# Loading an FFN weight as whole rows in two DMAs instead of four column pieces

## The chip, the cores and the metric

The kernel runs on one core of a Trainium2 chip. The metric is the time of one execution on the device in microseconds; before the change it is 184.65 us, the median of three runs (184.38 to 184.68). Beside those runs there is one profiled execution, of which the profile and the trace tell.

## What is computed

A linear attention with sketched features for 4 batches of 4 heads (1088 positions, 32 dimensions a head), and behind it a feed-forward network on the 4352 rows of 128 that come out of it:

```
phi(x) = outer(S1 x, S2 x), 64 features
num = phi(q) (phi(k)^T v);  den = phi(q) sum(phi(k)) + 1e-6
x   = num / den              # 4352 x 128
h   = max(x @ w_in, 0)       # w_in: 128 x 2048
out = (h * h) @ w_out        # w_out: 2048 x 128
```

All inputs and the output are float32. w_in and w_out are 1 MB each.

## The kernel before

The work is a stream of FFN units with the attention of the next positions worked in between. `FC` cuts the 4352 positions into ten column chunks (256, 384, 448, 448, five of 512, 256). A chunk has 16 blocks of 128 hidden columns; they are grouped into units of one or two blocks. For a unit, PE multiplies a 128 x 128 block of `w_in` with the chunk's `xT` (`ffn1`, L597, into a PSUM tile `pg`), ACT takes the maximum with zero (L609) into `gt`, ACT or DVE squares it (L620, L622) into `g`, and PE multiplies with a block of `w_o` and adds up in PSUM (`ffn2`, L641, tile `po`). The first unit reads blocks 0, so the first 128 columns of `w_in` and `w_o`.

The order of the main part is worked out when the kernel is built, by the class `_Order` from given durations. What comes before it, up to the first 256 positions of `xT`, is written out by hand, and so are the first loads. In that prologue:

- DMAs are issued by SP, one after the other, in the order of the code: k, q and v of the first batch, then (behind `load_q(nc.sync, 0, 256, 640)`) the weights, then the rest of q (`load_q(nc.sync, 0, 640, S)`), and then k, v and q of the second batch. Tiles are `kn`, `qn` and `vn`; a DMA of `vn` writes 32 partitions, one of `kn` or `qn` all 128. SP uses eight semaphores in turn, so a DMA is issued only when the eighth before it has landed.
- `w_in` comes from memory in four pieces of 512 columns (`load_wi`, L208), 128 partitions with 2 KB each, into `w_in32`. `w_o` comes in four pieces as well (`load_wo`, L213), each of 512 rows of `w_out`, put side by side on 128 partitions in runs of 512 bytes. The pieces alternate in the queue: w_in 0, w_in 1, w_o 0, w_in 2, w_o 1, w_in 3, w_o 2, w_o 3.
- POOL copies `w_in32` into `w_in`, in the type that PE reads, in four casts of 512 columns (`cast_wi`, L685). Each cast reads all 128 partitions of its columns. The casts stand in POOL's order behind its setup work and ahead of the small copies `rd` (L510) that the second part of the first batch needs.
- PE works through the sketch of k (`kf`, `kvp`), denominators and numerators of the first 256 positions (`den`, `num`), two small groups on tile `x`, one warm matmul that reads the first 512 columns of `w_in` (L835), and then the first four FFN matmuls (L597). DVE makes `xT` for them (L844).

```
    for c in range(4):
        cast_wi(c)
...
    for _ in range(W3):
        nc.tensor.matmul(st["warm"][:, :], w_in[:, 0:128], w_in[:, 0:512])
```

Of the kernel before, what the change touches and what calls it, by code (L numbers as in the profile page):

```python
# [14 lines left out]
def _ap(t: bass.AP, p0: int, np_: int, off: int, free):  # L15
    p = list(t.ap)[0]
    return bass.AP(
        t.tensor, t.offset + p0 * p[0] + off, [[p[0], np_]] + [list(d) for d in free]
    )
# [88 lines left out]
def kernel(  # L108
# [11 lines left out]
    nc = tc.nc  # L120
# [39 lines left out]
    def sb(name, cols, dt=F32, rows=128):  # L160
        return cpool.tile([rows, cols], dt, tag=name, name=name)
# [9 lines left out]
    w_in32, w_o, w_in = sb("w_in32", 2048), sb("w_o", 2048), sb("w_in", 2048, F32R)  # L171
# [14 lines left out]
    def load_q(eng, b, c0, c1):  # L186
        eng.dma_start(
            qn[b % 2][:, c0:c1],
            bass.AP(q.tensor, q.offset + b * H * S * D + c0, [[G * D, 128], [1, c1 - c0]]),
        )  # L190
# [13 lines left out]
            ),  # L204
        )

    def load_wi(eng, c):
        eng.dma_start(  # L208
            w_in32[:, 512 * c : 512 * c + 512], moe_w_in[:, 512 * c : 512 * c + 512]
        )  # L210

    def load_wo(eng, c):
        eng.dma_start(  # L213
            _ap(w_o, 0, 128, 512 * c, [[128, 4], [1, 128]]),
            bass.AP(
                moe_w_out.tensor, moe_w_out.offset + c * 512 * 128,
                [[128, 128], [128 * 128, 4], [1, 128]],
            ),
        )

# [484 lines left out]
        )  # L705
    nc.scalar.copy(ss[:, :], sp[:, 0:80])
    load_q(nc.sync, 0, 256, 640)
    load_wi(nc.sync, 0)
    load_wi(nc.sync, 1)
    load_wo(nc.sync, 0)  # L710
    load_wi(nc.sync, 2)
    load_wo(nc.sync, 1)
    load_wi(nc.sync, 3)
    for c in range(2, 4):
        load_wo(nc.sync, c)
    load_q(nc.sync, 0, 640, S)
    keep_warm(W1)
    a_kT0(0, 2)
# [348 lines left out]
    for u in range(NU):  # L1067
        ci, c0, n, d0, m = units[u]
# [93 lines left out]
```

## Time and profile before

| | |
|---|---|
| median of three runs | 184.65 us |
| profiled execution | 184.44 us, its span 182.6 us |
| PE busy | 177.6 us, 97% of the span |
| DVE, ACT, POOL busy | 67%, 74%, 21% |
| granted TensorE clock | 0.998 of full speed |
| DMA | 24610 packets, 11.26 MB |
| w_in, four DMAs of 256 KB | issue to landing 4.0 to 5.4 us, median 4.2 |
| w_o, four DMAs of 256 KB | issue to landing 4.9 to 6.1 us, median 5.6 |

Times in the profile are from the span's start. A busy PE is one with a matmul in its pipeline. In the row of tenths each digit is the busy share of one of 40 slices of 4.6 us. A line of the timeline gives start, length, engine, source line, operation, tile written and tile read, count, and in brackets how long the engine had been idle and what released it; several like instructions are merged. The timeline shows `w_in32` and `w_in` both as `w_in`, since buffer numbers are left out.

### The profile page before, as it was taken

Reading aid. Unit: us, or ns where it says so; the run is one execution under the profiler, and the core shown is the slowest. Engines: PE = TensorE matmul, PEld = TensorE weight load, DVE = VectorE, ACT = ScalarE, POOL = GpSimd, SP = SyncE. Lnnn points to the kernel's source line nnn. Section 1 sums busy time; section 2 is a strip of 40 time slices with the busy share of each in tenths; the row PEclk is TensorE's granted clock in tenths of the full one; section 3 lists DMA queues with packets and bytes.
Section 4 is the critical chain, followed back from the end, with each engine's and each line's share of the span. In section 5 each row is a group of like instructions: output and inputs, shape, how many; then the busy total and the mean of one; then the engine's idle time right before and its main releaser. Section 6 shows DMA issues by size and latency. Waiting matters only on the chain.

```text
span 182.6 us, 3995 instructions
## 1 busy us (share of the span) xinstructions
PE 177.6 (97%) x1529; PEld 104.7 (57%) x1529; DVE 122.2 (67%) x262; ACT 136.0 (74%) x258; POOL 39.2 (21%) x158
## 2 busy tenths in 40 slices
PE   8899999999999999999999999999999999999992
PEld 2768876755645655555455554545555555555792
DVE  3979969999999961799994335996353334333640
ACT  3339679749948886799937778894777777777990
POOL 5535418438300002570018100500000000000000
PEclk9999999999999999999999999999999999999999
DMA  5899994010029500000030200003003000300111
GB/s 155 220 266 341 221 266 105 4 32 0 0 47 260 157 0 4 4 2 0 0 54 15 43 0 5 0 0 59 0 4 57 0 0 5 52 0 0 32 29 29
DMA packets 24610, 11.26 MB, mean 62 GB/s; under 512 B 17936, under 2 KB 23056, under 8 KB 24592
## 3 DMA queue, kind: packets, MB, share of 16 engines
q1 hardware_dynamic: 24272, 10.89, 24.5%
q8 instruction: 12, 0.20, 0.5%
q10 hardware_dynamic: 320, 0.13, 0.3%
q14 instruction: 6, 0.05, 0.1%
HBM read 8.78 MB, written 2.23 MB: 60 GB/s over the span
## 4 chain that ended last, share of the span: by engine, by line
PE 95%; DMA 2%; DVE 0%; SPq 0%; issue 0%; ACT 0%; ACTq 0%
PE po L641 61%; PE pg L597 18%; PE nd L550 3%; PE po L636 2%; PE pol L636 2%; DMA kn<-in_k_dram 2%; PE qc L303 2%; PE nd L414 1%; PE kvp L396 1%; PE qc L347 1%; PE kvp L414 1%; PE x L756 1%; PE kf L315 0%; PE nd L347 0%; DVE kt L290 0%
## 5 line engine op out<-in xcount | busy, mean ns | idle before, releaser
L641 PE MATMUL po<-g,w_o 128*128 128x512 f32 (+3 forms) x288 | 122.7, 547 | 0.2 <-PE pg L597 0.2
L609 ACT ACTIVATE gt<-pg 128x512 f32<-128x512 f32 (+3 forms) x144 | 75.2, 570 | 31.5 <-PE pg L597 31.0
L641 PEld LDWEIGHTS po<-g,w_o 128*128 128x128 f32 x288 | 53.4, 189 | 32.3 <-issue 24.8
L597 PE MATMUL pg<-xT,w_in 128*128 128x512 f32 (+3 forms) x160 | 70.2, 519 | 0.0
L620 ACT ACTIVATE g<-gt 128x512 f32<-128x512 f32 (+2 forms) x102 | 60.7, 623 | 1.6
L622 DVE TENSOR_TENSOR g<-gt 128x512 f32<-128x512 f32 (+3 forms) x43 | 30.4, 708 | 39.5 <-ACT gt L609 38.8
L597 PEld LDWEIGHTS pg<-xT,w_in 128*128 128x128 f32 x160 | 29.2, 190 | 28.5 <-ACT gt L609 11.6
L510 POOL COPY rd<-rc 32x9 f32<-32x9 f32 (+2 forms) x80 | 19.5, 243 | 26.4 <-DVE rc L502 23.2
L456 POOL COPY kv<-kvt 32x64 f32<-32x64 f32 x48 | 12.7, 264 | 44.7 <-DVE kvt L433 42.5
L519 DVE STREAM_SHUFFLE qa<-qc 128x576 f32<-128x576 f32 (+2 forms) x20 | 11.8, 646 | 0.0
L534 DVE TENSOR_TENSOR qp<-qa,qb 128x576 f32<-128x576 f32 (+2 forms) x20 | 10.8, 602 | 0.0
L482 DVE STREAM_TRANSPOSE qt<-qc 128x576 f32<-128x576 f32 (+2 forms) x10 | 5.8, 608 | 6.0 <-PE qc L347 4.3
L367 DVE TENSOR_TENSOR kp<-fs 128x576 f32<-128x576 f32 x12 | 8.7, 742 | 0.0
L645 DVE STREAM_TRANSPOSE oT<-po 128x512 f32<-128x512 f32 (+3 forms) x9 | 5.9, 651 | 2.1 <-PE po L641 2.1
L550 PE MATMUL nd<-qp,kv 32*32 32x288 f32 (+2 forms) x320 | 6.6, 354 | 0.0
L519 DVE STREAM_SHUFFLE qb<-qc 128x576 f32<-128x576 f32 (+2 forms) x10 | 6.1, 649 | 0.0
L567 DVE TENSOR_TENSOR xT<-nd,bc 128x576 fp32r<-128x576 f32 (+2 forms) x10 | 5.6, 589 | 0.6 <-PE nd L550 0.5
L636 PE MATMUL po<-w_o,g 128*128 128x128 f32 x32 | 5.8, 279 | 0.0
L296 DVE STREAM_TRANSPOSE qT<-qn 128x192 f32<-128x192 f32 (+3 forms) x11 | 5.7, 549 | 0.0
L636 PE MATMUL pol<-w_o,g 128*128 128x128 f32 x32 | 5.7, 275 | 0.0
L560 DVE STREAM_TRANSPOSE bc<-rd 128x576 f32<-128x576 f32 (+2 forms) x10 | 5.6, 593 | 0.0
L550 PEld LDWEIGHTS nd<-qp,kv 32*32 32x32 f32 x320 | 2.9, 103 | 3.6 <-issue 2.4
(106 smaller groups left out, 89.8 us busy)
## 6 DMA issues: line engine op xcount, KB each, us to landing
kn<-in_k_dram SPq DMA_DIRECT2D x3, 544.0 KB, 8.8
qn<-in_q_dram SPq DMA_DIRECT2D x3, 544.0 KB, 8.7
vn<-in_v_dram SPq DMA_DIRECT2D x9, 144.0 KB, 6.4
w_in<-in_moe_w_in_dram SPq DMA_DIRECT2D x4, 256.0 KB, 4.2
w_o<-in_moe_w_out_dram SPq DMA_DIRECT2D x4, 256.0 KB, 5.6
out_dram<-oT SPq DMA_DIRECT2D x12, 64.0 KB, 1.9
out_dram<-oT SPq DMA_DIRECT2D x8, 56.0 KB, 1.8
out_dram<-oT SPq DMA_DIRECT2D x8, 48.0 KB, 1.8
```

The lines of the kernel that those rows point to most:

```text
L367: nc.vector.tensor_tensor(out=_ap(st[b, "kp"], 0, 128, 64 * NT * h, [[64, NT], [8, 8], [1, 8]]), in0=_ap(fs, 0, 128, o, [[32, NT], [1, 8], ...
L456: nc.gpsimd.tensor_copy(_ap(st[b, "kv"], 32 * c, 32, 64 * h, [[32, E], [1, 32]]), _ap(st["kvt"], 32 * h, 32, 0, [[64, E], [1, 32]]),)
L510: nc.gpsimd.tensor_copy(st[b, "rd", i0][32 * h : 32 * h + 32, n * c : n * c + n], st["rc"][32 * c : 32 * c + 32, n * h : n * h + n],)
L519: nc.vector.stream_shuffle(in_=banks(st[b, "qc", i0], 2 * x, 0, m), out=_ap(st[b, which, i0], 0, 128, 2 * m * x, [[m, 2], [1, m]]), mask=m ...
L534: nc.vector.tensor_tensor(out=st[b, "qp", i0, e][:, r], in0=st[b, f"qa{e}", i0][:, r], in1=st[b, "qb", i0][:, r], op=mult,)
L550: nc.tensor.matmul(nd[32 * h : 32 * h + 32, 512 * c : 512 * c + m], kv[r, o : o + 32], qp[r, m * h : m * h + m], start=(e == 0), stop=(e = ...
L597: nc.tensor.matmul(st["pg", u][:, n * i : n * i + n], w_in[:, 128 * (d0 + i) : 128 * (d0 + i) + 128], xT[:, c0 : c0 + n],)
L609: nc.scalar.activation(gt[:, 0:w], st["pg", u][:, 0:w], Relu)
L620: nc.scalar.activation(to, of, Square)
L622: nc.vector.tensor_tensor(out=to, in0=of, in1=of, op=mult)
L636: nc.tensor.matmul(po[x // 128][:, 0:128], g[:, x : x + 128], w, start=(d == 0), stop=(d == NB - 1),)
L641: nc.tensor.matmul(po[0][:, 0:n], w, g, start=(d == 0), stop=(d == NB - 1))
```

## The change

`w_in32` is loaded as whole rows: one DMA for partitions 0 to 79 and one for partitions 80 to 127, each with all 2048 columns (8 KB a row). Both stand ahead of all of `w_o`, which follows as two pieces of 512 rows and one of 1024. The four casts stay as they are. The weights so come in five DMAs instead of eight. In the built kernel the first cast waits for both DMAs of `w_in` and the other three casts wait for nothing more; the order of instructions on PE, DVE, ACT and POOL is the same.

```
-    def load_wi(eng, c):
+    def load_wi(eng, c, n=1):
+        r = slice(512 * c, 512 * (c + n))
+        for p in (slice(0, 80), slice(80, 128)):
+            eng.dma_start(w_in32[p, r], moe_w_in[p, r])
+
+    def load_wo(eng, c, n=1):
         eng.dma_start(
-            w_in32[:, 512 * c : 512 * c + 512], moe_w_in[:, 512 * c : 512 * c + 512]
-        )
-
-    def load_wo(eng, c):
-        eng.dma_start(
-            _ap(w_o, 0, 128, 512 * c, [[128, 4], [1, 128]]),
+            _ap(w_o, 0, 128, 512 * c, [[128, 4 * n], [1, 128]]),
             bass.AP(
                 moe_w_out.tensor, moe_w_out.offset + c * 512 * 128,
-                [[128, 128], [128 * 128, 4], [1, 128]],
+                [[128, 128], [128 * 128, 4 * n], [1, 128]],
             ),
         )
...
     load_q(nc.sync, 0, 256, 640)
-    load_wi(nc.sync, 0)
-    load_wi(nc.sync, 1)
+    load_wi(nc.sync, 0, 4)
     load_wo(nc.sync, 0)
-    load_wi(nc.sync, 2)
     load_wo(nc.sync, 1)
-    load_wi(nc.sync, 3)
-    for c in range(2, 4):
-        load_wo(nc.sync, c)
+    load_wo(nc.sync, 2, 2)
     load_q(nc.sync, 0, 640, S)
```

## The prediction

> **What bounds the kernel now.** I read the page's busy shares first, then the timeline of PE, POOL and DVE around the first FFN matmul, then the queue of SP's DMA issues, and last the rates of other loads later in the trace.
>
> The page:
>
> ```profile
> PE 177.6 (97%) x1529; PEld 104.7 (57%) x1529; DVE 122.2 (67%) x262; ACT 136.0 (74%) x258; POOL 39.2 (21%) x158
> ...
> PE   8899999999999999999999999999999999999992
> ...
> DMA  5899994010029500000030200003003000300111
> ```
>
> PE is busy for 97% of the span and from about 15 us on has no gap worth naming, so whatever moves the start of the FFN moves the end by the same amount. The DMA engines are full only in the first seven slices (to about 27 us), and there the weights are loaded. So the change is decided before 15 us. POOL and then PE in that stretch (start, length, engine, line, what):
>
> ```profile
> 10.43 1.35 POOL L685 CAST w_in<-w_in 128x512 fp32r<-128x512 f32 x2 [3.24 <-DMA w_in<-in_moe_w_in_dram]
> 13.42 0.61 POOL L685 CAST w_in<-w_in 128x512 fp32r<-128x512 f32 x1 [1.64 <-DMA w_in<-in_moe_w_in_dram]
> 15.19 0.61 POOL L685 CAST w_in<-w_in 128x512 fp32r<-128x512 f32 x1 [1.16 <-DMA w_in<-in_moe_w_in_dram]
> ```
>
> ```profile
> 12.30 0.49 PE L835 MATMUL warm<-w_in 128*128 128x512 f32 x1
> 12.64 0.70 PE L597 MATMUL pg<-xT,w_in 128*128 128x256 f32 x4
> ...
> 13.71 0.47 PE L597 MATMUL pg<-xT,w_in 128*128 128x256 f32 x2
> 14.41 0.67 PE L641 MATMUL po<-g,w_o 128*128 128x256 f32 x2 [0.22 <-PE pg L597]
> ```
>
> The first cast starts at 10.43, as soon as the first column chunk lands, and ends 0.61 later at 11.04. Its first reader on PE, the warm matmul, starts only at 12.30, because the matmuls before it in PE's order end at 12.37. The first FFN matmul at 12.64 waits for xT, which DVE ends at 12.53:
>
> ```profile
> 12.11 0.42 DVE L844 TENSOR_TENSOR xT<-num,bc 128x256 fp32r<-128x256 f32 x1
> ...
> 13.48 1.16 DVE L622 TENSOR_TENSOR g<-gt 128x256 f32<-128x256 f32 x2
> ```
>
> So w_in's first chunk has about 1.2 us to spare, and nothing on PE waits for w_in today. SP's queue of issues:
>
> ```profile
> 5.92 0.43 SPq L187 DMA_DIRECT2D qn<-in_q_dram  x1
> 6.40 0.90 SPq L208 DMA_DIRECT2D w_in<-in_moe_w_in_dram  x2
> 7.34 0.43 SPq L213 DMA_DIRECT2D w_o<-in_moe_w_out_dram  x1
> 7.82 1.40 SPq L208 DMA_DIRECT2D w_in<-in_moe_w_in_dram  x1
> ```
>
> **What is removed.** Eight weight DMAs become five, 0.43 to 0.51 us of SP's time each, so three of them save some 1.4 us of SP. This buys nothing: the transfers are served in order behind each other and DMA stays at 9 tenths, so the queue is never short of work. The loads behind the weights (qn from column 640, kn and vn of the second batch) are issued earlier, but stand behind the same bytes. They have slack: qn lands 6.1 us after its issue at 11.32, so at 17.4, and its transposes start at 19.50; kn lands at 20.7 and its transposes start at 21.62. I cost them at nothing. If the whole weight stream ended over 0.9 us later, kn would be the next late thing; the bytes are the same, so I do not expect it. The order on PE, DVE, ACT and POOL is unchanged.
>
> **What is added: one wait in place of four.** A row-wise DMA carries all columns of some partitions, and each cast reads all partitions, so the first cast now waits for both w_in DMAs, 1.05 MB, where it waited for one chunk of 0.26 MB. Behind it in POOL's queue stand only the other three casts (then nothing until the `rl` copies at 16.61). They run back to back, one every 0.74 us (two took 1.35). With T the landing of the second w_in DMA they end at about T + 0.66, 1.40, 2.14 and 2.88.
>
> How late may T be? The FFN matmuls of 256 columns follow each other every 0.12 us, so the warm matmul of 512 columns needs about 0.24 us of PE. With 0.1 us from a releaser to PE (xT's end at 12.53 to the matmul at 12.64) the first cast may end at 12.64 - 0.24 - 0.1 = 12.3 without cost, so T may be 12.3 - 0.66 = 11.64. Beyond that PE waits at the warm matmul, and everything behind it in PE's order (the four matmuls of `pg`, the sketch of q, the rest) is late by T - 11.64. The later casts do not add: chunks 1, 2 and 3 are first read at 13.71, 15.39 and 17.61, so with the delay they have until T + 2.07, 3.75 and 5.97.
>
> **When does T come?** The trace has no 8 KB rows and no load of 80 or 48 partitions, so I bound it, landing to landing. The load ahead of w_in is qn, issued at 5.92, landed 2.7 later, at 8.6. Behind it, 1.05 MB at three rates of this trace:
>
> ```profile
> 56.00:57.00 1.00, 1.00 (x4) 0.60 (x4) 0.96 (x3) 0.97 (x3) 0.00 (x0) 1.00 0.98 402
> 57.70:58.60 0.90, 0.90 (x4) 0.58 (x4) 0.90 (x2) 0.67 (x2) 0.00 (x0) 1.00 1.08 209
> 60.00:60.60 0.60, 0.60 (x4) 0.23 (x3) 0.60 (x3) 0.60 (x2) 0.00 (x0) 1.00 1.02 413
> ```
>
> These windows (last column GB/s) are later loads with no weights among them: kn, then vn, then qn. kn and qn cover 128 partitions with long rows and run at 402 and 413 GB/s. vn covers 32 partitions per DMA and falls to 209; its four DMAs, issued at 54.47, 54.89, 55.36 and 55.84, land 4.1, 4.4, 4.5 and 4.4 later, so the last three (410 KB) take from 58.6 to 60.25, 250 GB/s.
> - Fast end: at 425 GB/s (qn's 557 KB in the 1.3 us after vn's last landing), 1.05 MB take 2.5 us: T = 11.1.
> - vn's rate, 250 GB/s: 4.2 us, T = 12.8.
> - Slow end: today's first two chunks, 524 KB, land at 11.1 (issued at 6.87, 4.2 later), 2.5 us after qn, 210 GB/s: 5.0 us, T = 13.6.
>
> I take a little better than vn, 260 GB/s: 4.0 us, T = 12.6. vn is the nearest row because it is the only load here that leaves partitions out, and the two new DMAs do so too, though less (80 and 48 against 32); the long rows pull the other way, towards kn. Both ends stay in the range. Delay: 12.6 - 11.64 = 1.0 us.
>
> [...]
>
> **A small gain back.** Two DVE squares of one shape, 256 columns each, differ:
>
> ```profile
> L622 DVE TENSOR_TENSOR g<-gt x2: 413/618/824, 13.5 to 14.2; 128x256 f32<-128x256 f32 x2
> ```
>
> The first, 0.82 us from 13.48, lies beside the cast at 13.42 to 14.03; the second, beside no cast, takes 0.41. PE waited 0.22 us for the first (`po` at 14.41). With the change, the first FFN matmul is at T + 1.0 and this square, 0.84 later, at T + 1.84, in the third cast (to T + 2.14): it loses 0.3 us instead of 0.4 or more. The second then meets the fourth cast, but its reader (15.15 today, against its end at 14.64) has 0.5 to spare. I take 0.1 us of gain, between none and 0.22.
>
> **Sum.** +1.0 - 0.1 = +0.9 us. The profiled execution took 184.44 us, 182.6 of span and 1.84 around it, which does not change: 185.34. It lies 0.21 under the median of the runs, 184.65, so the median comes to 185.5. PE's later work passes the delay on whole, as it has no gaps that could swallow it.
>
> **Rivals.**
> - *Not slower: the long rows are fast.* If the 1.05 MB land within 3.0 us of qn (345 GB/s or more), T is at most 11.64 and the wait is hidden as today's is. For it: kn and qn run at 402 and 413 GB/s, and from 7.8 to 9.6 us, with almost only w_in's 2 KB pieces in the queue, the load moved 218 GB/s, so the column pieces themselves may be what is slow. Against it: neither DMA covers the 128 partitions that kn and qn do. Time: 184.65 less 0 to 0.22, that is 184.4 to 184.65; to be faster by more than 0.37 us the earlier end of the casts would have to help the q chain on DVE too, whose `pd` (15.23) stood beside the fourth cast, and PE behind it has little to give. [...]
> - *Slower still: T at 13.2 or later.* The row-wise form keeps today's 210 GB/s, or one of the DMA engines lags (an instruction fetch shares them; the third w_in issue took 1.40 instead of 0.43), and the first cast now waits for the last engine of both DMAs. That T does come at today's rate is also what happens if the 8 KB rows are cut into 2 KB packets. T = 13.6 gives +1.96 - 0.1: 186.5.
> - *w_o becomes the wait.* Its first quarter now stands behind all of w_in. At 250 GB/s it lands at T + 1.05, and its first reader (14.41 plus the delay) comes at T + 2.77. It would decide only if the quarter took 2.8 us, under 100 GB/s; the half that is loaded last has 4 us of cover. Chance 2 in 100, counted with the slower case.
>
> **How the numbers follow.** 0.2% is 0.37 us, about what a measurement of this kernel can tell. My case, T from 12.1 to 13.2 (+0.4 to +1.5 us): 0.48. Slower still: 0.22. Not slower: 0.30, of which 0.20 lies within 0.37 us and 0.10 below. So slower 0.70, same 0.20, faster 0.10. The range goes from the fast end, 184.4, to the slow end and a little, 186.8.
>
> **What would show it.** In the profile after: the first cast starts at T, at 12.6 (12.1 to 13.2), with its wait of 3.2 us grown to about 5.4, and the other three follow without a wait; the warm matmul on w_in starts some 0.7 us behind the first cast's start instead of at 12.30, and PE has a new gap of about 1 us just before it; xT still ends near 12.5; the first square on DVE is shorter than 0.82. Packets fall from 24610 by 512 and rise by 128, to 24226. From 20 us on, each FFN matmul is late by the same 0.9. I am wrong if the first cast starts before 11.7 (no loss), if PE waits at `po` for w_o, or if kn's transposes at 21.62 begin to wait for their load.

## The result, and the profile after

The changed kernel takes 190.48 us (median of 6, 189.64 to 190.96) against 184.47 for the kernel before (6 runs): a ratio of 1.0315, 95% interval 1.0284 to 1.0347. That is 6.0 us slower; forecast were 0.9 us and a range up to 186.8. The direction was right, the size was not. The profiled execution took 190.94 us, its span 189.2. In three of the kernels below the profiled execution was a slow one (188.09, 207.91 and 467.26 us, against medians of 185.47, 185.71 and 186.75), so no time is read from those three profiles, only when loads landed and what had to wait for them.

The page after (busy shares, PE's tenths, the granted clock in tenths, the packets, the chain by line):

```profile
PE 180.4 (95%) x1529; PEld 107.2 (57%) x1529; DVE 121.7 (64%) x262; ACT 136.4 (72%) x258; POOL 38.7 (20%) x158
...
PE   8955999999999999999999999999999999999992
...
PEclk9996699999999999999999999999999999999999
...
DMA packets 24178, 11.26 MB, mean 60 GB/s; under 512 B 17888, under 2 KB 23008, under 8 KB 24032
...
PE po L641 59%; PE pg L597 18%; DMA w_in<-in_moe_w_in_dram 5%; PE nd L550 3%; PE po L636 2%; PE pol L636 2%; DMA vn<-in_v_dram 2%; PE qc L303 2%; PE nd L414 1%; PE qc L347 1%; PE kvp L414 1%; SPq L199 1%; PE warm L831 0%; PE nd L347 0%; POOL w_in L685 0%; ACTq L221 0%
```

PE has a hole in slices three and four (9.5 to 18.9 us), w_in's DMA now stands on the chain with 5%, and the clock row, all nines before, has two sixes right behind the hole. POOL and PE at that place in the timeline, the line numbers of the written-out prologue four lower than before on PE:

```profile
15.81 2.28 POOL L685 CAST w_in<-w_in 128x512 fp32r<-128x512 f32 x4 [8.62 <-DMA w_in<-in_moe_w_in_dram]
```

```profile
12.04 0.50 PE L440 MATMUL x<-kvt,irep 32*128 32x128 f32 x8 [0.34 <-ACT sw L826]
16.47 0.79 PE L831 MATMUL warm<-w_in 128*128 128x512 f32 x1 [3.93 <-POOL w_in L685]
17.07 1.06 PE L597 MATMUL pg<-xT,w_in 128*128 128x256 f32 x4
```

The first cast starts at 15.81 instead of 10.43. PE waits 3.93 us at the warm matmul, and the first FFN matmul comes at 17.07, 4.43 us late. But the FFN is later than that in the end: matched one to one, the matmuls from 22 us on start 6.34 us after their counterparts of before, and it stays so to the end. The other 1.9 us arise between 17 and 22 us. Three windows after (the columns behind the engines are the granted clock, the DMA share and GB/s) show why:

```profile
12.40:15.70 3.30, 0.14 (x8) 0.00 (x0) 0.59 (x2) 0.37 (x1) 0.00 (x0) 1.00 1.13 256
15.75:22.58 6.83, 6.11 (x49) 5.00 (x50) 4.64 (x23) 4.07 (x8) 4.02 (x13) 0.50 1.07 296
22.60:30.00 7.40, 7.40 (x127) 6.04 (x125) 4.42 (x12) 4.91 (x10) 1.44 (x8) 1.00 0.92 232
```

In the first PE is idle. In the second, 6.83 us long, it works at a granted clock of 0.50; only then is the clock back at 1.00.

So there are two losses: w_in lands late, and PE is slow after the wait. The experiments split the first and test the second.

### The profile page after: what moved, and what is told of

It is laid out like the page before. It is cut to its first block, busy times and chain, and to the rows that moved or that the text cites. A ratio compares the mean times of both kernels' runs of the same rounds, so it can differ in the third digit from the quotient of the medians.

```text
span 189.2 us, 3993 instructions
## 1 busy us (share of the span) xinstructions
PE 180.4 (95%) x1529; PEld 107.2 (57%) x1529; DVE 121.7 (64%) x262; ACT 136.4 (72%) x258; POOL 38.7 (20%) x158
## 2 busy tenths in 40 slices
DMA packets 24178, 11.26 MB, mean 60 GB/s; under 512 B 17888, under 2 KB 23008, under 8 KB 24032
## 4 chain that ended last, share of the span: by engine, by line
PE 89%; DMA 6%; SPq 1%; POOL 0%; ACTq 0%; issue 0%; DVE 0%; POOLq 0%
PE po L641 59%; PE pg L597 18%; DMA w_in<-in_moe_w_in_dram 5%; PE nd L550 3%; PE po L636 2%; PE pol L636 2%; DMA vn<-in_v_dram 2%; PE qc L303 2%; PE nd L414 1%; PE qc L347 1%; PE kvp L414 1%; SPq L199 1%; PE warm L831 0%; PE nd L347 0%; POOL w_in L685 0%; ACTq L221 0%
## 5 line engine op out<-in xcount | busy, mean ns | idle before, releaser
L641 PE MATMUL po<-g,w_o 128*128 128x512 f32 (+3 forms) x288 | 124.0, 552 | 0.0
L641 PEld LDWEIGHTS po<-g,w_o 128*128 128x128 f32 x288 | 54.4, 193 | 31.9 <-issue 24.5
L597 PE MATMUL pg<-xT,w_in 128*128 128x512 f32 (+3 forms) x160 | 71.8, 531 | 0.0
L597 PEld LDWEIGHTS pg<-xT,w_in 128*128 128x128 f32 x160 | 30.6, 199 | 28.6 <-ACT gt L609 11.5
```

The source lines that it names most:

```text
L597: nc.tensor.matmul(st["pg", u][:, n * i : n * i + n], w_in[:, 128 * (d0 + i) : 128 * (d0 + i) + 128], xT[:, c0 : c0 + n],)
L641: nc.tensor.matmul(po[0][:, 0:n], w, g, start=(d == 0), stop=(d == NB - 1))
```

## The experiments

All are made from the changed kernel unless said otherwise, and compared with the kernel before on the same chip, whose median was 184.29 to 184.68 us. Kernels measured on different chips are compared by their ratios. For landings I use the trace's increments of a DMA's semaphore, one per DMA engine: "fifteen engines" is the last of all but the latest.

**Whole rows in one DMA.**

```
-        for p in (slice(0, 80), slice(80, 128)):
+        for p in (slice(0, 128),):
```

> The changed kernel with w_in's whole rows in one DMA over all 128 partitions instead of 80 and 48. Theory A (a DMA that leaves partitions out moves slowly, whatever its rows): the rows run at kn's rate, 345 to 425 GB/s behind qn, w_in lands at 11.1 to 12, the first cast starts there instead of at 15.8, PE has no gap before the warm matmul, the granted clock stays at 1.0, and the time is 184.4 to 185.0 us. Rival B (8 KB rows as such are slow, in a DMA of any shape): the first cast still starts at 14.5 or later and the time is 188.5 to 190.5 us. Rival C (it is the order, w_in whole ahead of the casts): first cast at 13 to 14, time 186 to 188 us.

Measured: 187.31 us, ratio 1.0140 (1.0117 to 1.0164). The rows are the same 8 KB, but w_in lands on fifteen engines at 11.45 and on the last at 12.58, against 14.32 and 15.69 with 80 and 48. An 8 KB packet takes 0.309 us at the median, against 0.553. Theory B, that long rows are slow as such, is refuted, and theory A holds for fifteen engines. Its time does not: the sixteenth engine is 1.13 us behind, and after a wait of only 0.78 us at the warm matmul the clock falls here too. The time is in the range of rival C, but the cast at 12.64 is not, and the order by itself, tested below, is worth 0.1% or nothing. PE's waits and the window behind them:

```profile
PE warm L831 <- POOL w_in L685: 0.8, 1, 0.8
```

```profile
14.00:18.00 4.00, 4.00 (x46) 3.18 (x45) 3.75 (x16) 3.08 (x7) 1.68 (x7) 0.58 1.09 321
```

**Two DMAs of 64 and 64.**

```
-        for p in (slice(0, 80), slice(80, 128)):
+        for p in (slice(0, 64), slice(64, 128)):
```

> The changed kernel with the two row-wise DMAs of 64 and 64 partitions instead of 80 and 48. Theory A: partitions 0 to 63 and 64 to 127 are each served at about the rate of vn's DMAs (230 to 250 GB/s), so the two take 2.1 to 2.3 us each, one after the other; w_in lands for most engines near 13 and for the last one near 14 to 15.5, time 188 to 190.5 us. [...] Rival B (8 KB rows as such): same as the changed kernel, 190 to 191 us.

Measured: 189.78 us, ratio 1.0273 (1.0224 to 1.0321), packets 0.581 us. With equal halves an 8 KB packet takes no less than with 80 and 48 (0.553), so the unequal split is not what makes it slow. w_in lands on fifteen engines at 14.38, later than the 13 that vn's rate gave.

**Three DMAs, the first across the middle.**

```
-        for p in (slice(0, 80), slice(80, 128)):
+        for p in (slice(32, 96), slice(0, 32), slice(96, 128)):
```

> The row-wise load in three DMAs: partitions 32 to 95, then 0 to 31, then 96 to 127. The first has as many rows as the first DMA of the 64/64 run (64), but from both halves of the partitions. Theory A1 (what counts is whether a DMA reaches both the lower and the upper 64 partitions): its 64 rows land for most engines at 9.7 to 10.3 and for the last near 11, an issue to landing of 4.2 to 4.8 us against 5.8 for partitions 0 to 63; the two DMAs of 32 behind it are slow (1.1 us each); first cast at 13 to 14, time 187.5 to 189 us. Theory A2 (what counts is the number of partitions in a DMA): the first DMA takes as long as partitions 0 to 63 do, issue to landing 5.6 to 6.0 us, and the first cast starts at 14.5 or later, 189.5 us or more.

Measured: 189.34 us, ratio 1.0288 (1.0256 to 1.0321). This tells the number of partitions from their place. Both this kernel's first DMA and that of the 64/64 run have 64 rows. Issue to landing of the DMAs on w_in, first of this kernel, then the 64/64 run; in both the shortest is the first DMA:

```profile
DMA to landing us min/median/max: 6.9/7.0/7.2
```

```profile
DMA to landing us min/median/max: 5.8/6.7/7.6
```

Read to the last engine, partitions 32 to 95 (6.9) look worse than 0 to 63 (5.8), against theory A1. But 6.9 is one engine, at 13.24. The other fifteen land at 10.00 to 11.50, half of them by 10.3, those of the 64/64 run at 10.19 to 12.02, half by 11.6. In the packets it is plainest: once running, those of partitions 32 to 95 take 0.309 us like those of the full DMA, and those of the two DMAs of 32 partitions behind it 0.44 and 0.57 at the median. So with 64 rows it is the place that counted (0.309 us a packet across the middle, 0.581 with a half on each side), as in A1; the time that I gave for it missed, since I had not counted the late engine.

**The split by itself, with columns again** (eight DMAs; the first cast waits for two of them).

```
-    load_wi(nc.sync, 0, 4)
+    for c in range(4):
+        load_wi(nc.sync, c)
```

> The other half of the change alone: the split into 80 and 48 partitions, but by column pieces again (eight DMAs of 512 columns, all ahead of w_o), so that the first cast waits for the first two only. Theory (the partial DMAs slow the whole of w_in, but the loss reaches PE only since the first cast waits for all of it): the last of w_in lands at 13 to 15, as in the changed kernel, the first two pieces of 256 KB at 10.5 to 11.6; first cast under 11.7, time 184.4 to 185.5 us with at most a short gap at the first matmul on w_o. Rival (runs of 8 KB are what is slow in the changed kernel, not the split): all of w_in lands by 12.5.

Measured: 185.71 us, ratio 1.0063 (1.0043 to 1.0083). The last of w_in lands at 14.55, as late as expected, yet the first cast starts at 10.80 and costs nothing: PE waited for the slow form only where the first cast waits for all of it (3.93 us in the changed kernel). The time misses the range by 0.2. Of the 1.4 us of loss, about 0.5 is at the first matmul on w_o, which now stands behind eight DMAs: PE waits 0.75 us there, where it waited 0.22 before. The rest I did not trace. The landings come from loads, which do not wait for PE.

**Order alone** (four column pieces of 128 partitions, all ahead of w_o).

```
-    load_wi(nc.sync, 0, 4)
+    for c in range(4):
+        load_wi(nc.sync, c)
```

(with `load_wi` as it was before, the pieces of w_o as in the change)

> The kernel before with only the order of the change: four pieces of w_in by columns, all ahead of w_o, which follows as two quarters and a half. Theory A (the order is harmless, the row-wise DMAs are the loss): the first cast starts at 10.4 to 10.8, the casts of chunks 2 and 3 by 13, no new wait on PE, time 184.2 to 184.8 us. Rival C (w_o behind all of w_in is late for the first matmul on it at 14.41, or the merged half of w_o is): a gap at that matmul, time 185 to 187 us.

Measured: 184.89 us, ratio 1.0010 (0.9984 to 1.0037). Moving w_o back costs little. The gap of rival C is there, in small (PE's waits; at this matmul it waited 0.22 us before the change):

```profile
PE po L640 <- DMA w_o<-in_moe_w_out_dram: 0.8, 1, 0.8
```

**Two halves by columns**, 128 partitions and 4 KB runs.

```
-    load_wi(nc.sync, 0, 4)
+    load_wi(nc.sync, 0, 2)
+    load_wi(nc.sync, 2, 2)
```

(with `load_wi` as before, over n pieces)

> w_in in two DMAs of 1024 columns over all 128 partitions (4 KB runs) ahead of w_o, which follows as in the changed kernel. Theory: runs of 4 KB over all partitions move at the rate of the single DMA, so the first half lands at 10.2 to 11.2 with the late engine, under the 11.64 that cost nothing, and the second by 12.7, ahead of its first reader at 15.4: no new gap on PE, the granted clock stays 1.0, time 184.2 to 184.8 us, at best 0.2 us under the kernel before. Rival: w_o's first quarter, now behind all of w_in, is late for its matmul at 14.41 as in the run with four column pieces first (0.5 us): 184.9 to 185.4 us.

Measured: 184.88 us, ratio 1.0018 (0.9993 to 1.0044). The first cast starts at 11.31 and PE does not wait for it, only 0.27 us for w_o at the matmul that the rival names. The clock stays at 1.00, and nothing is gained: w_in's earlier end has no one who needs it. The time lies between the ranges of theory and rival. This form is not told apart from the kernel before.

**PE kept busy through the wait.**

```
+    keep_warm(18)
     for _ in range(W3):
         nc.tensor.matmul(st["warm"][:, :], w_in[:, 0:128], w_in[:, 0:512])
```

> The changed kernel with 18 more matmuls on constants (512 columns of bf16 each, some 0.21 us each, their result is not used) between PE's last matmul on tile x and the warm matmul on w_in, so that PE is busy while it waits. Theory: of the 6 us lost, 4.05 us are the wait for w_in and some 2 us are FFN work at the lower granted clock (0.58 and 0.74 from 15 to 25 us) that follows PE's idle 4 us. Then the first cast still starts at 15.8, the granted clock stays at 1.0 and the time is 188.3 to 188.8 us. Rival (the lower clock costs nothing, since ACT or DVE set the pace after 17 us, and the whole loss is the wait): time within 0.5 us of 190.5.

Measured: 189.31 us, ratio 1.0248 (1.0225 to 1.0271). The first cast starts at 15.53, hardly earlier, but the clock row is nines throughout, and from 16 to 33 us of the old timeline the FFN matmuls are 4.04 us late instead of 6.34. The same window as in the changed kernel:

```profile
15.75:22.58 6.83, 6.83 (x68) 5.34 (x67) 4.99 (x24) 5.25 (x11) 4.16 (x15) 1.00 1.07 266
```

So the lower clock costs about 2.3 us. The two starts are not quite alike: w_in lands 0.28 us sooner here, and the warm matmul starts only when the added ones are done (16.57), not as soon as the cast ends (16.14). In the time only 1.2 us of the 2.3 appear, so the theory's 188.3 to 188.8 is missed: near 41 us PE stops once for about 0.5 us in the middle of `nd` with nothing to wait for,

```profile
PE nd L550 <- issue: 0.5, 1, 0.5
```

behind which the FFN stays 0.7 us later. I take it for a side effect of the added PE instructions; that was not tested.

**The same in the kernel with one DMA**, where the wait is short: four matmuls instead of 18.

> The kernel with w_in in one DMA over 128 partitions, and four more matmuls on constants (512 columns of bf16, 0.21 us each) on PE ahead of the warm matmul on w_in, which fill the 0.8 us that PE waits there. Theory: that wait alone, 0.8 us, makes the granted clock fall to half for 3.4 us and costs 1.2 us of the 2.6; filled, the clock stays at 1.0 and the time is 185.6 to 186.3 us. Rival: so short a wait does not move the clock, which fell for PE's thin work before it; it falls again, 187.0 to 187.6 us.

Measured: 185.82 us, ratio 1.0072 (1.0052 to 1.0092). Without them the ratio is 1.0140, so they are worth 0.7%, 1.3 us; matched one to one, the FFN is 0.91 us later than before with them and 2.2 us later without. The same window as above, with 0.58 there, has 1.00 here:

```profile
14.00:18.00 4.00, 4.00 (x54) 3.22 (x53) 3.54 (x18) 3.79 (x8) 1.55 (x7) 1.00 1.08 327
```

The wait of 0.78 us of PE at this place is thus dearer in its clock (1.3 us) than in itself.

**The late engine.** In the changed kernel and in the kernels with one and with three DMAs, one DMA engine lands w_in 0.8 to 1.4 us behind the other fifteen (0.2 with 64 and 64, where the others are late themselves). In the profiles with unshifted instructions a fetch of 16 KB of instructions, one packet of 0.9 to 1.3 us, starts at 7.9 to 8.7 us, just as w_in begins. I took that for the cause and moved the fetch, first in the kernel with one DMA:

```
-    keep_warm(W0)
+    keep_warm(8 * W0, 64)
...
-    keep_warm(W1)
+    keep_warm(8 * W1, 64)
```

> The kernel with w_in in one DMA over 128 partitions, and PE's two groups of warm matmuls at the start cut into eight times as many of 64 columns (40 and 24 instead of 5 and 3 of 512), so that PE's instruction stream is 112 instructions longer ahead of w_in at about the same PE time. Theory: the one DMA engine that lands 1.1 us behind the other fifteen (12.58 against 11.04 to 11.45) is the one that carries a 16 KB instruction fetch at 7.9 us, taken 0.9 to 1.3 us; with more instructions ahead the fetch comes at 5.5 to 7 us, before w_in's bytes, the last engine lands w_in at 11.5 to 11.8, the first cast starts there instead of at 12.64, and the time falls from 187.3 to 184.6 to 185.6 us. Rival: that engine is late for another cause; the first cast stays at 12.4 to 12.8 and the time at 186.9 to 187.6 us.

Measured: 185.47 us, ratio 1.0068 (1.0050 to 1.0087), by the ratios 1.3 us better than without the shift, within the range of the theory. But the profile does not show its mechanism: the fetch came at 6.03 as planned, and the last engine landed 0.2 us behind the next instead of 1.13, yet all of them landed later (up to 12.90); the issue of w_in's DMA, beside the fetch, took 1.26 us instead of 0.43. In the four other runs the mean clock was 0.998 to 1.000, where the kernel with one DMA has 0.991 in all four: the gain, as large as that of filling the wait, may be the clock's. Then with a further shift (twelve more matmuls) and PE's wait filled:

> The kernel with w_in in one DMA over 128 partitions, with the small warm matmuls at the start (40 and 36 of 64 columns, 136 PE instructions more than before) and the four constant matmuls that fill PE's wait. In the run with 112 more the profiled fetch came at 6.0 us and met the issue of the w_in DMA (1.26 us instead of 0.43), so this one moves it further, to 5 to 5.9 us. Theory (the late DMA engine is the one that carries PE's instruction fetch): w_in lands on the last engine at 11.3 to 11.8, less than 0.6 us behind the others, the first cast starts by 11.9, the clock stays at 1.0, and the time is 184.4 to 185.2 us, against 185.8 with the filling alone. Rival (late for another cause): first cast at 12.3 to 12.6 again, 185.6 to 186.2 us.

Measured: 186.75 us, ratio 1.0114 (1.0082 to 1.0147), slower than with the filling alone. The theory's time is missed, and its landings too: with the fetch at 6.97, w_in lands on fifteen engines at 11.71 and on the last at 14.37, 2.66 us behind. And in the changed kernel itself:

> The changed kernel itself (80 and 48 partitions) with the earlier fetch and with eleven constant matmuls in PE's wait. If the three causes add up (partial DMAs, one late engine, the lower clock), the first cast starts at 13.9 to 14.6 instead of 15.8, the clock stays at 1.0, and the time is 186.9 to 187.9 us: the partial DMAs alone, 2.5 to 3.3 us over the kernel before. Rival (the late engine is late because of the partial DMAs, not the fetch): first cast at 15.3 to 15.8, and 188.3 to 189.3 us.

Measured: 189.29 us, ratio 1.0302 (1.0242 to 1.0362), first cast at 15.89. The sum of three causes is refuted in this form; the time is the rival's, though the rival's reason does not hold for the kernel with one DMA, which has no partial DMAs and a late engine all the same. PE still waits, and yet the clock stays at 1.00 in this profile:

```profile
16.55 0.50 PE L832 MATMUL warm<-w_in 128*128 128x512 f32 x1 [1.02 <-POOL w_in L685]
```

The fetch moved to 6.60, but the late engine did not go away: it was late sooner. qn, ahead of w_in, landed on fifteen engines at 8.61 and on the sixteenth at 11.25, 2.6 us behind, and w_in at 14.14 and 15.76. The lag begins with the fetch in the profiles of both settings (in the changed kernel with the fetch at 8.68, in this one at 6.60), which speaks for it, but no run in which it was moved landed w_in sooner. Nor does the lag belong to whole rows: the first column piece of the run with the order alone lands at 9.90 on fifteen engines and at 10.68 on the last. Its cause stays open.

## Why the prediction was wrong

- *What bounds it, and where the change is decided:* right. The first cast waits for both DMAs and the three others follow without a wait (2.28 us for four), PE gets one new gap, just before the warm matmul, and what it loses there goes to the end undiminished. The loads behind the weights, though, were not all issued earlier: kn came at 15.11 instead of 11.87.
- *How late T may be, 11.64:* right. Two kernels show it while their clock is still at 1.00: with one DMA T is 12.58, 0.94 past it, and the second to fourth FFN matmuls start 0.94 to 0.95 late; with three DMAs T is 15.25, 3.61 past it, and they start 3.60 to 3.63 late. In the changed kernel it makes 15.69 - 11.64 = 4.05 us. That its FFN starts 4.43 late is the clock already, at which the warm matmul takes 0.79 instead of 0.49.
- *When T comes, 12.6, at most 13.6:* this is the step that failed first. T was 15.69. From the landing of qn on the slowest engine (9.39) it took 6.3 us, 166 GB/s, under my slow end of 210. That end was today's rate of w_in, a row in which every DMA covers all 128 partitions, so it was no bound for DMAs that don't. T came 2.1 us after the slow end of 13.6: 1.37 of it is the late engine, and the other 0.7 is that on fifteen engines qn ended at 8.98 instead of 8.6 and w_in then moved at 196 GB/s. I then moved the one fitting row, vn's, upwards from 250 to 260 because of the long runs and because 80 is more than 32. In the three-DMA run the place decided where the count was the same (0.309 us a packet for partitions 32 to 95, 0.581 for halves of 64). Split by the runs, of the 4.05 us the partial DMAs are 2.87 (14.32 against 11.45 on fifteen engines) and the late engine, whose own cause is open, 1.37 (15.69 - 14.32), less the 0.19 by which one full DMA would have been in time on fifteen engines (11.64 - 11.45).
- *vn's rate for DMAs that leave partitions out, 250 GB/s:* too good, also in what I expected of the 64/64 run. There the two halves took from qn's landing, about 8.3, to 14.38 on fifteen engines, 6.1 us or 172 GB/s.
- *"184.44 plus the delay":* the sum had no term for the clock at all, though a PE that waits was in the forecast. This is the second error, 2.3 us. My own 1 us of wait could have met it too: in the run with one DMA 0.78 us of wait cost 1.3 us of clock. The trace of before could not show it, as its clock row is nines throughout. After the change the stretch at 0.50 is 6.83 us long, with one DMA 3.41, and there PE was busy for 2.29 of the 3.41 us just before the fall.
- *The small gain back:* right in kind, larger than taken. The two squares are 0.42 us each at 18.1 and 18.4 (0.82 and 0.41 before); the first starts as the last cast ends (18.09), not in the third cast. With the clock held up the delay shrinks behind the first FFN matmul by 0.3 us (4.35 to 4.04 with 18 constant matmuls, 1.22 to 0.91 with one DMA and four), but by 0.1 with eleven (4.25 to 4.14), against my 0.1.
- *Rivals:* "slower still" was the right one in kind (slow rate, and one lagging engine, both named) and far too small, 186.5. w_o did not become the wait, and kn's transposes did not wait either. Packets are 24178, 48 under the forecast of 24226: that is sixteen for each of the three DMAs fewer, and the kernel with one DMA has sixteen fewer again (24162).

## What to carry to other kernels

A DMA that loads whole rows of some partitions is not the same load cut differently: here an 8 KB packet took 0.55 to 0.58 us at the median with 80 and 48 or with 64 and 64 rows, where one DMA over all partitions took 0.309. Everything that reads across partitions then waits for the last group (the first cast until 15.81), while a cut by columns keeps the early first piece (10.80 with the same 80 and 48). A wait put in front of a busy PE is to be priced twice, as the wait and as the slow stretch that may follow it; with 0.78 us of wait the clock stood at 0.50 for 3.41 us, and the second was the larger (1.3 us). And a bound taken from "the nearest rows" is one only if the rows share what is changed: the slow end came from loads of the very kind that the change gave up.

## What the runs showed of the hardware that I had not expected

- The granted clock fell to 0.50 for 3.41 us or for twice that, and the length of PE's wait did not set which: 3.41 us with a wait of 0.78 (one DMA) and of 3.42 (three DMAs), 6.83 us with 2.61 (64/64) and 3.93 (the changed kernel), and no fall with 1.02 behind eleven constant matmuls (all in the profiled executions). Where it fell, the FFN lost from its first matmul on a further 1.2, 0.9, 1.4 and 1.9 us, in that order. Nor is it fixed for a kernel: the one with three DMAs has a mean clock of 0.991 in its profiled execution, as for one fall of 3.41, and 0.982 in the three others, as for 6.83. What sets it these runs do not show.
- An 8 KB packet into partitions 32 to 95 took 0.309 us at the median once running, into 0 to 63 and 64 to 127 about 0.58.
- One of the sixteen DMA engines lands w_in 0.8 to 1.4 us after the others in the changed kernel and in those with one or three DMAs, and in the changed kernel loads behind w_in are late on one engine too (qn's rest lands on fifteen at 17.58 and on the last at 19.09, kn at 19.28 and 22.07, vn's first at 19.99 and 22.74).
- SP was held up long at an issue: that of qn's rest took 5.01 us at 10.05 after the change, against 0.50 before. It was long without a slow load ahead of it too: 2.80 us with w_in in one DMA and 3.29 with the four column pieces first. What holds it up was not tested.
